# Integer exponentials in groups of four heads from the ninth period on, kept in the space of used-up weights

## The chip, the cores and the metric

One core of a Trainium2 chip runs the whole program. The metric is the device time of one execution in microseconds (us). Engines are named as in the profile: PE (TensorE, with its weight loads as PEld), DVE (VectorE), ACT (ScalarE), POOL (GpSimd), SP (SyncE, which issues DMAs).

## The reference

Two attentions over the same 2048 tokens, mixed by a gate per token (32 heads of 16, bfloat16 inputs):

```python
g = sigmoid((x * gate_w).sum(-1, keepdims=True))      # x: 1 x 2048 x 512
a = A_ref(x, A_wqkv, A_wo)      # full softmax attention
b = B_ref(x, B_wqkv, B_wo)      # 8 keys per query: s, s-2, ..., s-14
return g * a + (1 - g) * b
# A: qkv = x @ wqkv; p = softmax(q k^T * 16**-0.5); o = p v; o @ wo
# B: the same over the 8 gathered keys; keys before token 0 are masked
```

## The kernel before

**Branch A** is the bulk: 32 heads x 2048 x 2048 exponentials. The work goes in periods: a chunk of 512 queries times a group of four heads, 4 x 8 = 32 periods (the last one is split in two halves, so 33 entries). A period has 64 blocks of 128 keys by 512 queries, one head each. PE forms the scores of a block in PSUM (`ring`, two buffers of 3 and 2 blocks), ACT takes the exponential of 3 or 2 blocks at once into `pT`, and PE multiplies `pT` with the values into the period's accumulator (`acc`), where an extra column of ones sums the denominators. The four heads of a period use four 32-wide strips of the PE array, so products for different heads run side by side.

**Blocks on DVE.** In each period `n_dve` of the 64 blocks (3 to 16, 12 in periods 8 to 26) do not go to ACT. PE puts their scores into a shared PSUM bank (`dq`), DVE turns them into 16-bit integers that, read as bfloat16, are a piecewise linear exponential (`p1`, one instruction per block into the tile `dt`), and three more integer instructions per group of blocks add 32, 64 and 96 to those integers (`sh`, from `dt` into `pd_a`). PE multiplies all four versions with differently weighted values (`dpv`: `vp_all` for the first, `vd_all` for the others), which corrects the linear error. The constants: `NV` = 4 versions, `NGR` = 3 blocks in a group, `NGF` = 4 blocks from period `FLAT0` = 27 on, `NPD` = 3 buffers of `pd_a`, `NDL` = 3 buffers of `dt`, `LATE0` = 8 the period from which the late buffers of `dt` are used.

The passes `sh` have two forms. In a group of three the destination rows are padded (`ROW` = 514 columns for 512) and the source is read in half rows: 1536 columns. From period 27 on source and destination are contiguous: 2048 columns in one run (`flat`). The integers lie in `dt_a` in the early periods, in `dt_a` and two parts of `wkv` (A's key and value weights, used up by then) in periods 8 to 26, and in three parts of `bw` (B's weights) from period 27 on, where the first groups wait for the last projections out of `bw` (`bw_users`).

**Branch B** works in 16 tiles of 128 tokens (`b_tile`). PE projects keys, values and queries out of `bw`; SP stores keys and values in DRAM (`kv_scr`) and loads them back shifted (`ksh`, `vsh`); POOL multiplies and sums the logits (`prod`, `lg`); DVE finds the maximum and the sum of the exponentials, ACT the exponentials; POOL scales them, multiplies with the values and adds up (`av`, `obb`), partly by accumulating DMAs from its own queue. PE transposes `obb` (`fin`), DVE stores it in `obt`, and the output projection takes `obt` and A's `oat` together. POOL also divides A's results by their denominators (`rden`, `ott`).

**The order.** Every piece of work is an `Op` with an engine, a planned duration, a due time and its dependences. `list_schedule` plays a timetable with these durations, picks at each step what is due first among what can start, and the instructions of all engines are emitted in that order; each engine then keeps its order on the chip and waits by semaphores. Durations may have parts marked `True`: those occupy a port that the plan shares between DVE and POOL, one at a time. A POOL operation is (0.14 us, then some 0.5 us on the port); a padded pass is entirely off the port; a contiguous pass is given by `PT`. Results of POOL are planned with 4 us of margin before PE uses them and 3 us before DVE or ACT does (`MARGIN`). `BT` are the due times of B's tiles: `b_start`, then a step of `b_space` each. PE's gaps are filled with products of zeros (`zeros`).

Every engine's calls go through one helper, so the profile shows line 370 for nearly all operations and line 379 for the matmuls; the tiles' names tell them apart.

Of the kernel before, what the change touches and what calls it, by code (L numbers as in the profile page):

```python
# [12 lines left out]
BF16 = mybir.dt.bfloat16  # L13
# [6 lines left out]
    n_dve=(3, 3, 6, 6, 9, 9, 12, 12) + (12,) * 19 + (16,) * 4 + (8, 4),  # L20
    dve_tiles=4,
    b_start=36.0,
    b_space=(43.0,) * 16,
    chain=("pe", "dve", "act", "pool", "sp"),
)

# [1 line left out]
DH = 16  # L28
NG = 8
W = 8  # L30
DIL = 2
QW = 512
NEG = -1.0e9
FLAT0 = 27
BITS = 128.0
LN2 = 0.6931471805599453
SHIFT = 175.0
# [1 line left out]
NV = 4  # L39
NGR = 3  # L40
NGF = 4
NK1 = 2
# [7 lines left out]
NDE = 1  # L50
NDL = 3
# [57 lines left out]
PVU, PVN = 100.0, 4  # L109
GP = lambda kind, n: [(False, PRE), (True, NS[kind] * n)]  # L110
SB = lambda n: [(True, 0.065 + n / 3840.0)]
PT = lambda n: [(True, 0.1 + n / 3840.0)]
TT = lambda n: [(True, 0.075 + n / 960.0)]
PASS, SWITCH, KEEP, RIDE, ALONE = 0.22, 0.1, 1.2, 50.0, 3.0
WAIT, FREE, LATE, CLAMP = 0.15, 0.1, 10.0, -1.0
# [192 lines left out]
def kernel(  # L308
# [19 lines left out]
    DC = D // 128  # L328
# [6 lines left out]
    const = ctx.enter_context(tc.tile_pool(name="const", bufs=1))  # L335
# [95 lines left out]
    for pi in range(NP):  # L431
        first_unit.append(nu)
        n = n_dve[pi]
        gr = group_of(pi)
# [16 lines left out]
    for pi, (own, groups) in enumerate(seq):  # L451
        n = sum(len(g) for g in groups)
# [22 lines left out]

    wkv = const.tile([128, DC, 2 * D], BF16, name="wkv")
    wq = const.tile([128, DC, D], BF16, name="wq")
    wq2 = const.tile([128, DC, 8, 2, DH], BF16, name="wq2")
    q_scr = tc.dram_tile([NG * NC // 2 * 16, DH * QW], BF16, name="q_scr")
    wk3 = const.tile([128, DC, NK1, 2, DH], BF16, name="wk3")  # L480
    a_w3 = A_wqkv.rearrange("(c p) n -> p c n", p=128)
    wkp = const.tile([128, DC, (NG - NK1) // 2, 4, 2, DH], BF16, name="wkp")
    gw = const.tile([128, DC], BF16, name="gw")
    bw = const.tile([128, DC, 3 * D], BF16, name="bw")
    bwo = const.tile([128, DC, D], BF16, name="bwo")
# [22 lines left out]
    wkv_l = wkv[:].rearrange("p c n -> p (c n)")  # L508
    dt_bufs = [dt_a[:, k_ * NGR * QW:(k_ + 1) * NGR * QW] for k_ in range(NDE)]
# [319 lines left out]
    for h0, h1, pn in ((4, 8, 1), (8, 16, 2), (16, 24, 4), (24, 32, 6)):  # L829
        TB = 512 // ((h1 - h0) * DH)  # L830
        for tb in range(0, NT, TB):
            late = tb + TB > NT - NTD
# [3 lines left out]
    qt_tiles, o_q, q_tok, last_q = {}, {}, {}, [None]  # L836
# [120 lines left out]
    a = None  # L957
    for sc in range(NC):
        a = op("pe", 0.9, zmm(sc), GT + sc, full=1, deps=[o_bw, a] + o_xt[sc], alloc=[tzp] if sc == 0 else [],
               use=[tzp] if sc else [], rel=20.0)  # L960
    a = op("act", 0.25, zsig, GT + 5, deps=[a], use=[tzp])
    o_g = op("dve", 0.8, zgate, GT + 6, deps=[a])
    a = op("pe", 1.2, zrows, GT + 8, full=1, deps=[o_g, o_init_p], alloc=[tzr])
    o_gr = op("dve", 0.12, zcopy, GT + 9, deps=[a], use=[tzr])


    o_kvd, o_obt, bw_users = [], [], []
    obt_tiles, obt_tok = {}, {}
    WP = WH // 2
    HB = D // 2  # L970
# [1 line left out]
    def b_tile(t):  # L972
# [27 lines left out]
        a = op("pe", WAVE(2), proj("pk", 1, 0), tb - 34 - KB, full=2, deps=[o_bw] + o_xt[cb], alloc=[tk, tkv], rel=rel)  # L1000
        a = op("pe", WAVE(2), proj("pk", 1, 2), tb - 33.5 - KB, full=2, deps=[a], use=[tk])
        ka = op("dve", 0.61, ke, tb - 33 - KB, deps=[a], use=[tk, tkv])
        tk = tok("misc", 2)
        a = op("pe", WAVE(2), proj("pv", 2, 0), tb - 32 - KB, full=2, deps=[o_bw] + o_xt[cb], alloc=[tk], rel=rel, after=[a])
        a = op("pe", WAVE(2), proj("pv", 2, 2), tb - 31.5 - KB, full=2, deps=[a], use=[tk])
# [4 lines left out]

        def qe():
            V.tensor_scalar(out=st["qb"][:], in0=st["pq"][:], scalar1=float(DH) ** -0.5, scalar2=None, op0=ALU.mult)
        bw_users.append(a)
        tk = tok("misc", 2)
        a = op("pe", WAVE(2), proj("pq", 0, 0), tb - 24 - QB, full=2, deps=[o_bw] + o_xt[cb], alloc=[tk, tqb], rel=rel)
        a = op("pe", WAVE(2), proj("pq", 0, 2), tb - 23.5 - QB, full=2, deps=[a], use=[tk])
        bw_users.append(a)
        qa = op("dve", 0.61, qe, tb - 23 - QB, deps=[a], use=[tk, tqb])

        def load(key, off, hf):  # L1020
# [154 lines left out]
        for g_ in range(len(halves)):  # L1175
# [5 lines left out]
        a = op("dve", 0.34, sm_pre, tb + SMD, deps=[l1], use=[tlg])  # L1181
        a = op("dve", 0.0, sm_sub, tb + SMD, deps=[a], use=[tlg], parts=TT(H * W)) if SM_V else op(
            "pool", 0.0, sm_sub, GFIRST, deps=[a], use=[tlg], parts=GP("ff", H * W))
        a.lat += 0.0 if SM_V else 3.0
        l1.lat += SM_LAT[0]
        a = op("act", 0.36, sm_exp, tb + SMD, deps=[a], use=[tlg], lat=0.36 + SM_LAT[2])
        a = op("dve", 0.72, sm_post, tb + SMD, deps=[a], use=[tlg])
# [122 lines left out]
                pv_run(pend[q_:min(n, q_ + 4)], tn)  # L1310
            del pend[:n]

    bw_l = bw[:].rearrange("p c n -> p (c n)")
    wkv_users = [o for o in ops if o.eng == "pe" and o.name.startswith(("kp", "vp"))]
    d_st, d_last, d_sh = {}, [None, None], []
    d_count, d_ends = [0, 0, 0, 0], []
# [1 line left out]
    def d_set(pi, gi, t, j, qk_, tn):  # L1318

        c_, i = periods[pi]  # L1320
        late = pi >= LATE0
        flat, gr = pi >= FLAT0, group_of(pi)
        key = (pi, gi)
        first = key not in d_st
        if first:
            slot = d_count[3] % NDL if flat else d_count[0] % NDL if late else d_count[2] % NDE
            d_count[3] += flat
            d_count[0] += late and not flat
            d_count[2] += not late
            d_st[key] = dict(dt=bw_l[:, slot * gr * QW:(slot + 1) * gr * QW] if flat else dt_bufs[slot],  # L1330
                             td=tok("dtf", NDL) if flat else tok("dtl", NDL) if late else tok("dt", NDE), js=[], ts=[], p1=[])
        g = d_st[key]
        n_ = len(g["js"])
        g["js"].append(j)
        g["ts"].append(t)

        st = {}
        tx = tok("misc", 2)

        def dq():  # L1340
            st["x"] = misc_ps([128, QW])
            for t_, cs in parts_of(pi, t):
                mm(st["x"][:, cs], kt_all[32 * j:32 * j + 32, i, t_ * 128:(t_ + 1) * 128], qt_tiles[pi][32 * j:32 * j + 32, q_cols(pi)],
                   True, True, tile_position=(32 * j, 0))

        def p1():
            V.tensor_scalar(out=g["dt"][:, n_ * QW:(n_ + 1) * QW].bitcast(U16), in0=st["x"][:], scalar1=float(DH) ** -0.5 * BITS / LN2,
                            scalar2=(127.0 + DEXP + SHIFT * float(DH) ** -0.5 / LN2) * BITS, op0=ALU.mult, op1=ALU.add)
        deps = [o_q[pi], o_k[i][tiles_of(pi, t)[0] // TPC]] + [o_vd[(4 * i + j, t_)] for t_ in tiles_of(pi, t)]
        if first and flat and d_count[3] <= NDL:  # L1350
            deps += bw_users
        elif first and late and d_count[0] <= NDL:
            deps += wkv_users + d_ends[-NV * NDE:]
        a = op("pe", 0.0, dq, tn - 3.0, mode="r", js=[j], deps=deps, alloc=[tx] + ([g["td"]] if first else []),
               use=[q_tok[pi]] + ([] if first else [g["td"]]), after=[qk_, d_last[1]], ride=True, name=f"dq{pi}")
        d_last[1] = a
        o = op("dve", 0.61, p1, tn + P1D, deps=[a], use=[tx, g["td"]], after=[d_last[0]], name=f"p1_{pi}")
        d_last[0] = o
        g["p1"].append(o)
        if len(g["js"]) < gr:  # L1360
            return
        vs = [o_vd[(4 * i + j_, t2)] for t_, j_ in zip(g["ts"], g["js"]) for t2 in tiles_of(pi, t_)]

        def sh(m, pb):
            def s():
                o_, i_ = pb.bitcast(U16)[:, :, 0:QW], g["dt"].bitcast(U16)
                if not flat:
                    i_ = _ap(i_, [list(i_.ap[0]), [QW // 2, 2 * NGR], [1, QW // 2]])
                else:
                    o_ = o_.rearrange("p q n -> p (q n)")  # L1370
                V.tensor_scalar(out=o_, in0=i_, scalar1=STEP * m, scalar2=None, op0=ALU.add)
            return s

        def pv(m, pb):
            def s():
                pv_mm(pi, [(t_, j_, pb[:, n1, 0:QW]) for n1, (t_, j_) in enumerate(zip(g["ts"], g["js"]))],
                      lambda t2: vd_all[:, m - 1, t2 - (NT - NTD)] if m else vp_all[:, t2])
            return s

        def dpv(m, pb, deps, use, dl):  # L1380
            b = op("pe", 0.0, pv(m, pb), dl, mode="c", js=g["js"], full=1, deps=deps + [o_t0[pi]] + vs,
                   use=[use, acc_tok[pi]], name=f"dpv{pi}")
            o_pv[pi].append(b)
            d_ends.append(b)
        dpv(0, g["dt"].rearrange("p (q n) -> p q n", q=gr), list(g["p1"]), g["td"], tn + 4.5)
        for m in range(1, NV):
            pb = pd_bufs[d_count[1] % NPD]
            if flat:
                k0 = d_count[1] % NPD * gr * QW
                pb = pd_a[:, k0:k0 + gr * QW].rearrange("p (q n) -> p q n", q=gr)  # L1390
            d_count[1] += 1
            tp = tok("pd", NPD)
            a = op("dve", 0.0, sh(m, pb), tn + 1.5 + SHD * (m - 1), deps=list(g["p1"]), alloc=[tp], use=[g["td"]],
                   lat=(0.065 + NGR * QW / 1920.0 if not flat else 0.1 + gr * QW / 3840.0) + SH_LAT, after=d_sh[-1:],
                   parts=[(False, 0.065 + NGR * QW / 1920.0)] if not flat else PT(gr * QW), name=f"sh{pi}")
            d_sh.append(a)
            dpv(m, pb, [a], tp, tn + 4.5 + SHD * m)

    pend, dwait = [], []
    for k, us in enumerate(sets):  # L1400
        ring = "rA" if k % 2 == 0 else "rB"
        n = len(us)
# [211 lines left out]
```

## Time and profile before

| | |
|---|---|
| median of 3 runs | 800.21 us (799.62 to 801.82) |
| profiled execution: time | 803.18 us |
| profiled execution: span, first to last instruction | 800.3 us |
| busy: PE, DVE, ACT, POOL | 741.5, 692.6, 774.5, 644.3 us |
| mean granted TensorE clock | 0.998 |
| ACT: exponentials of branch A, 128x1536 and 128x1024 | 337 at 1538 ns, 336 at 1117 ns |
| DVE: padded passes of 128x1536 / contiguous of 128x2048 | 288 at 940 ns / 57 at 744 ns |
| POOL: last sum of branch B | starts at 722.2 us |
| ACT: last exponential | ends near 793 us |

Durations of ACT overlap a little, since an instruction starts before the one ahead of it has ended; busy time counts the overlap once. A group's mean can mix shapes, where the profile says so. A wait is put down to the last semaphore that came.

### The profile page before, as it was taken

The numbers are of one execution on the slowest core, as the hardware profiler recorded it, in microseconds if no ns is written. First come the engines' busy times: TensorE is split into PE (matmuls) and PEld (weight loads), VectorE is DVE, ScalarE is ACT, GpSimd is POOL, SyncE is SP. The second block draws the span as 40 slices with busy tenths as digits, with TensorE's granted clock in tenths as the row PEclk, the third lists the DMA queues.
The fourth block names the chain that finished last, engine by engine and source line by source line (L and its number), as shares of the span: only waits on it lengthen the run. The fifth ranks groups of instructions, "written<-read, shape, count | busy, mean of one in ns | idle before, by whom it ended". The sixth has DMA issues, their size and how long they took to land.

```text
span 800.3 us, 17773 instructions
## 1 busy us (share of the span) xinstructions
PE 741.5 (93%) x6817; PEld 241.9 (30%) x6876; DVE 692.6 (87%) x1100; ACT 774.5 (97%) x697; POOL 644.3 (81%) x1067
## 2 busy tenths in 40 slices
PE   8999989999999999999999999998999999999997
PEld 4333333233222222222222232232232232222233
DVE  5638787998887899999998899899898999988986
ACT  3999999999999999999999999999999999999996
POOL 4098989899999997899989899999989999991000
PEclk9999999999999999999999999999999999999999
DMA  8413071625344535336352626253625371100000
GB/s 265 115 46 106 21 177 47 156 64 128 98 113 118 131 83 143 81 97 142 73 146 77 162 74 165 66 117 112 144 65 109 107 169 35 47 8 20 2 2 28
DMA packets 58886, 77.21 MB, mean 96 GB/s; under 512 B 3744, under 2 KB 50848, under 8 KB 58800
## 3 DMA queue, kind: packets, MB, share of 16 engines
q1 hardware_dynamic: 52608, 53.91, 21.6%
q0 software_dynamic: 6048, 22.02, 14.8%
q8 instruction: 53, 0.87, 0.4%
q14 instruction: 33, 0.27, 0.1%
q10 hardware_dynamic: 144, 0.13, 0.0%
HBM read 43.78 MB, written 10.26 MB: 68 GB/s over the span
## 4 chain that ended last, share of the span: by engine, by line
ACT 50%; PE 23%; issue 22%; DVE 4%; DMA 1%; SPq 0%; ACTq 0%; DVEq 0%
ACT pT L370 49%; PE misc_ps L379 15%; PE ring L379 7%; DVE pd_a L370 1%; DMA xld<-in_A_x_dram 1%; DVE dt_a L370 1%; ACT lg L370 1%; DVE vd_all L370 1%; DVE wkv L370 0%; DVE kt_all L370 0%; PE pxt L647 0%; DVE vp_all L370 0%; DVE ssum L370 0%; DVE rr L370 0%; DVE osb L370 0%
## 5 line engine op out<-in xcount | busy, mean ns | idle before, releaser
L370 ACT ACTIVATE pT<-ring 128x1536 bf16<-128x1536 f32 (+1 forms) x674 | 766.5, 1327 | 10.5 <-PE ring L379 7.3
L379 PE MATMUL ring<-qt,kt_all 32*128 32x512 bf16 (+1 forms) x1736 | 265.5, 375 | 41.3 <-ACT pT L370 32.8
L379 PE MATMUL misc_ps<-pT,vp_all 128*17 128x512 bf16 (+3 forms) x1736 | 201.9, 377 | 0.3 <-DVE dt_a L370 0.2
L370 POOL TENSOR_TENSOR prod<-ksh,qb 128x256 f32<-128x256 bf16 x256 | 175.7, 757 | 30.0 <-DMA ksh<-kv_scr 27.2
L379 PEld LDWEIGHTS <-kt_all 32*128 32x128 bf16 x2112 | 92.2, 91 | 291.2 <-issue 281.6
L370 POOL TENSOR_TENSOR prod<-prod 128x256 f32<-128x256 f32 (+1 forms) x256 | 172.8, 690 | 5.9
L370 DVE TENSOR_SCALAR pd_a<-wkv 128x1536 uint16<-128x1536 uint16 x150 | 137.2, 940 | 1.0 <-PE misc_ps L379 0.6
L379 PE MATMUL misc_ps<-qt,kt_all 32*128 32x512 bf16 (+1 forms) x376 | 130.5, 374 | 3.8 <-DVE dt_a L370 2.2
L379 PE MATMUL misc_ps<-pd_a,vd_all 128*17 128x512 bf16 (+1 forms) x1128 | 131.1, 375 | 0.5 <-DVE pd_a L370 0.4
L379 PE MATMUL misc_ps<-z 128*32 128x512 bf16 x382 | 127.9, 388 | 1.6 <-DVE z L370 1.6
L370 DVE TENSOR_SCALAR pd_a<-dt_a 128x1536 uint16<-128x1536 uint16 x138 | 126.5, 939 | 0.6
L370 DVE TENSOR_SCALAR wkv<-misc_ps 128x512 uint16<-128x512 f32 x150 | 100.1, 681 | 18.5 <-PE misc_ps L379 17.6
L370 DVE TENSOR_SCALAR dt_a<-misc_ps 128x512 uint16<-128x512 f32 x138 | 92.1, 682 | 21.0 <-PE misc_ps L379 19.6
L370 POOL TENSOR_TENSOR prod<-vsh,lg 128x256 f32<-128x256 bf16 x128 | 84.1, 772 | 0.0
L379 PEld LDWEIGHTS <-vp_all 128*17 128x17 bf16 (+1 forms) x2112 | 55.9, 88 | 84.8 <-issue 71.9
L370 POOL TENSOR_TENSOR av<-vsh,lg 128x256 f32<-128x256 bf16 x128 | 80.0, 664 | 0.0
L370 DVE TENSOR_SCALAR bw<-misc_ps 128x512 uint16<-128x512 f32 x76 | 50.8, 684 | 10.8 <-PE misc_ps L379 10.2
L379 PE MATMUL misc_ps<-bw,xT 128*128 128x512 bf16 x163 | 50.6, 384 | 1.9 <-issue 1.4
L379 PEld LDWEIGHTS <-vd_all 128*17 128x17 bf16 x1128 | 34.9, 88 | 53.4 <-issue 46.6
L379 PEld LDWEIGHTS <-z 128*32 128x32 bf16 x382 | 32.9, 96 | 45.5 <-issue 26.5
L370 DVE TENSOR_SCALAR pd_a<-bw 128x2048 uint16<-128x2048 uint16 x57 | 41.2, 744 | 0.1
L370 POOL TENSOR_TENSOR rden<-rden,g_rw 128x16 f32<-128x16 f32 x30 | 9.3, 310 | 37.5 <-DVE rden L370 37.4
(100 smaller groups left out, 596.0 us busy)
## 6 DMA issues: line engine op xcount, KB each, us to landing
ksh<-kv_scr SPq DMA_DIRECT2D x32, 512.0 KB
vsh<-kv_scr SPq DMA_DIRECT2D x32, 512.0 KB
av<-prod POOLq DMA_DIRECT2D x28, 512.0 KB, 6.2
av<-av POOLq DMA_DIRECT2D x14, 512.0 KB, 5.0
kv_scr<-kvs SPq DMA_DIRECT2D x16, 256.0 KB
qt<-q_scr SPq DMA_DIRECT2D x30, 128.0 KB
out_dram<-osb SPq DMA_DIRECT2D x15, 128.0 KB
xld<-in_A_x_dram SPq DMA_DIRECT2D x3, 512.0 KB
```

The lines of the kernel that those rows point to most:

```text
L370: return chain_on(key, f(*a, **k))
L379: return chain(nc.tensor.matmul(out, lhsT=lhsT, rhs=rhs, start=start, stop=stop, **kw))
```

## The change

Periods 8 to 26 now work as those from 27 on did: their 12 blocks make three groups of four instead of four groups of three, and their passes are contiguous. `FLAT0` becomes 8. The integers of these and of all later groups lie in three parts of 2048 columns: two in `wkv`, which fill it, and one in a new tile `wx`, which holds what were `wq2` and `wkp` (copies of A's query and key weights) one behind the other. `bw` is no longer used for this, and the wait for its last users goes; the first three groups wait instead for the last projections out of A's weights, for the queries of period 1, and for the last early groups. `n_dve` is unchanged. The plan's cost `PT` of a contiguous pass changes from 0.633 us, all on the shared port, to 0.5 us off it and 0.25 us on it. The steps between B's due times become 45 us instead of 43 after the fourth tile.

```diff
-    b_space=(43.0,) * 16,
+    b_space=(43.0,) * 4 + (45.0,) * 12,
...
-FLAT0 = 27
+FLAT0 = 8
...
-PT = lambda n: [(True, 0.1 + n / 3840.0)]
+PT = lambda n: [(False, 0.5), (True, 0.25)]
...
-    wq2 = const.tile([128, DC, 8, 2, DH], BF16, name="wq2")
+    n_q2, n_kp = DC * 8 * 2 * DH, DC * (NG - NK1) // 2 * 8 * DH
+    wx = const.tile([128, n_q2 + n_kp], BF16, name="wx")
+    wq2 = wx[:, 0:n_q2].rearrange("p (c h e d) -> p c h e d", c=DC, h=8, e=2)
+    wkp = wx[:, n_q2:n_q2 + n_kp].rearrange("p (c i j e d) -> p c i j e d", c=DC, i=(NG - NK1) // 2, j=4, e=2)
...
-    wkp = const.tile([128, DC, (NG - NK1) // 2, 4, 2, DH], BF16, name="wkp")
...
-    bw_l = bw[:].rearrange("p c n -> p (c n)")
+    dt_flat = [wkv_l[:, 0:NGF * QW], wkv_l[:, NGF * QW:2 * NGF * QW], wx[:, 0:NGF * QW]]
...
-            d_st[key] = dict(dt=bw_l[:, slot * gr * QW:(slot + 1) * gr * QW] if flat else dt_bufs[slot],
+            d_st[key] = dict(dt=dt_flat[slot] if flat else dt_bufs[slot],
...
-        if first and flat and d_count[3] <= NDL:
-            deps += bw_users
-        elif first and late and d_count[0] <= NDL:
-            deps += wkv_users + d_ends[-NV * NDE:]
+        if first and late and d_count[3 if flat else 0] <= NDL:
+            deps += wkv_users + [o_q[1]] + d_ends[-NV * NDE:]
```

The lines that collected `bw_users` in `b_tile` go as well.

More of the change, by code (lines that the diff above doesn't have):

```diff
@@ L964 @@
     o_gr = op("dve", 0.12, zcopy, GT + 9, deps=[a], use=[tzr])
-    o_kvd, o_obt, bw_users = [], [], []
+    o_kvd, o_obt = [], []
     obt_tiles, obt_tok = {}, {}
@@ L1012, in qe @@
             V.tensor_scalar(out=st["qb"][:], in0=st["pq"][:], scalar1=float(DH) ** -0.5, scalar2=None, op0=ALU.mult)
-        bw_users.append(a)
         tk = tok("misc", 2)
@@ L1016, in b_tile @@
         a = op("pe", WAVE(2), proj("pq", 0, 2), tb - 23.5 - QB, full=2, deps=[a], use=[tk])
-        bw_users.append(a)
         qa = op("dve", 0.61, qe, tb - 23 - QB, deps=[a], use=[tk, tqb])
```

## The prediction

> **What bounds the kernel now.** I read the busy times first, then the costliest groups, then the busy time by stretch. From the page:
>
> ```profile
> PE 741.5 (93%) x6817; PEld 241.9 (30%) x6876; DVE 692.6 (87%) x1100; ACT 774.5 (97%) x697; POOL 644.3 (81%) x1067
> ...
> L370 ACT ACTIVATE pT<-ring 128x1536 bf16<-128x1536 f32 (+1 forms) x674 | 766.5, 1327 | 10.5 <-PE ring L379 7.3
> ...
> L370 DVE TENSOR_SCALAR pd_a<-wkv 128x1536 uint16<-128x1536 uint16 x150 | 137.2, 940 | 1.0 <-PE misc_ps L379 0.6
> ...
> L370 DVE TENSOR_SCALAR pd_a<-dt_a 128x1536 uint16<-128x1536 uint16 x138 | 126.5, 939 | 0.6
> ...
> L370 DVE TENSOR_SCALAR pd_a<-bw 128x2048 uint16<-128x2048 uint16 x57 | 41.2, 744 | 0.1
> ```
>
> ACT computes the exponentials (674 instructions) and almost never waits. The three pd_a groups are the integer passes on DVE: 288 of 1536 columns at 940 ns, 57 contiguous ones of 2048 at 744 ns. The last kind is what the change spreads. By first starts, the changed stretch (periods 8 to 26) runs from about 228 us to 684.7, where the first contiguous pass stands. Busy time by stretch (PE, PEld, DVE, ACT, POOL, then granted clock):
>
> ```profile
> 228.00:684.00 456.00, 423.94 (x3648) 129.12 (x3683) 420.15 (x621) 454.54 (x411) 421.72 (x708) 1.00 0.44 110
> 684.00:708.00 24.00, 22.09 (x212) 7.03 (x205) 22.18 (x32) 23.95 (x23) 23.01 (x30) 1.00 0.08 27
> 708.00:724.00 16.00, 15.47 (x123) 3.80 (x123) 12.55 (x22) 14.97 (x14) 14.57 (x21) 0.89 0.03 10
> 724.00:793.00 69.00, 64.91 (x776) 23.65 (x779) 61.16 (x106) 69.00 (x62) 2.33 (x4) 1.00 0.03 7
> ```
>
> ACT is busy 454.54 of 456 us where the change acts; from 228 to 793 its idle time sums to 1.46 + 0.05 + 1.03 + 0 = 2.5 us. The number of exponentials stays, so 2.5 us is about all there is to win. POOL (branch B) is the other full engine: 421.72 of 456, until it ends near 723. What is added to POOL moves its end, or stops those who wait for it.
>
> **What a contiguous pass does to POOL.** Only 684 to 724 has both at once. One POOL multiply in 228 to 684.5, and then in 684.5 to 721 (behind the bar: busy us, mean ns):
>
> ```profile
> L370 POOL TENSOR_TENSOR av<-vsh,lg 128x256 f32<-128x256 bf16 x88 | 53.4, 647 | 0.0
> ```
> ```profile
> L370 POOL TENSOR_TENSOR av<-vsh,lg 128x256 f32<-128x256 bf16 x8 | 7.1, 926 | 0.0
> ```
>
> Those eight on the timeline (start, us), and DVE beside them:
>
> ```profile
> 698.04 7.13 POOL L370 TENSOR_TENSOR av<-vsh,lg 128x256 f32<-128x256 bf16 x8
> ```
> ```profile
> 698.60 0.68 DVE L370 TENSOR_SCALAR pd_a<-bw 128x2048 uint16<-128x2048 uint16 x1
> ...
> 699.80 3.23 DVE L370 TENSOR_SCALAR pd_a<-bw 128x2048 uint16<-128x2048 uint16 x3
> ```
>
> A fifth pass starts at 703.54. Eight multiplies take 8 x 647 = 5.18 us undisturbed and 7.13 here: 1.95 over five passes, 0.39 us each; by the means, 8 x (926 - 647) = 2.23, 0.45 each. Over all 16 passes until 721, with every POOL row's mean set against its own of before (12 adds at 799 against 734, and so on), the excess is about 5.3 us, 0.33 each. I take **0.40 us of POOL per pass**, between 0.33 and 0.45, because the changed stretch is as dense in POOL work as this one. The 1536-column passes cost POOL nothing visible: the 647 ns was measured among them.
>
> The same passes from DVE's side, until 721 and after it (minimum/median/maximum ns):
>
> ```profile
> L370 DVE TENSOR_SCALAR pd_a<-bw x16: 629/916/1130, 684.7 to 719.7; 128x2048 uint16<-128x2048 uint16 x16
> ```
> ```profile
> L370 DVE TENSOR_SCALAR pd_a<-bw x41: 629/683/695, 724.0 to 791.0; 128x2048 uint16<-128x2048 uint16 x41
> ```
>
> With POOL at work a pass takes 0.9 us, without it 0.68.
>
> The Trainium skill, SBUF — State Buffer, "Who interferes with whom", says that a VectorE instruction in a two-port mode and a GpSimd instruction lock each other out of a shared port pair, and that the loser is blocked for the whole instruction. The trace agrees on who waits, not on the size: by the page a pass would cost POOL its whole 0.68 us, and the sum below would grow by 171 x 0.28 = 48 us; the rows show 0.33 to 0.45.
>
> **The change part by part.** *Passes on DVE.* Periods 8 to 26 hold 19 x 12 = 228 blocks: 76 groups of three now, 57 groups of four after, three passes each. Out go 228 x 0.940 = 214 us, in come 171 x 0.90 = 154 us: DVE is relieved of 60 us. None of it is on the path, since ACT does not wait there.
>
> *Products on PE.* A group's four products take one turn of the array each, with three or with four heads side by side: 76 x 4 turns become 57 x 4, 76 fewer. On the timeline such turns follow each other by 0.22 us (737.80, 738.02, 738.24), so PE is freed of 17 us in 456. Its reach is the 2.5 us of ACT's idle time, and part of that has other causes; I book 0.
>
> *Bits in wkv and wx instead of dt_a, wkv and bw.* The first groups wait for the last projections out of wkv and wx. Those are done in the first periods, and passes out of wkv already run from 245 us: 0. The group of four gathers one block more before its passes start; its tiles come in threes as before: 0, and if the three buffers were short, some tenths of a us at a wait now 0.6 us in all ("pd_a<-wkv ... 0.6").
>
> *b_space.* The due times of tiles 5 to 15 move later, by 2 us a tile, 22 us for the last. They order the queues (its projections on PE, its DMAs on SP, its chain on POOL) but hold nothing back, as POOL is full anyway. Cost 0 by themselves, since an output of the last quarter has until 793.
>
> *Contention on POOL.* 171 x 0.40 = **68 us** more POOL work (56 to 77), in an engine with 34 us idle in 456. Of that idle time 7.8 us are waits for its own summing DMAs and 5.7 its own chain; waits for DVE (rden 4.6, mx 3.1, qb 2.0, rr 0.9) sum to 10.6, of which DVE's relief may give back some 3.
>
> *What the order foresees.* All queues are written from one plan, and each engine keeps its order. Up to now the plan charged a contiguous pass 0.633 us of the shared port, more than the 0.33 to 0.45 of the trace; the new PT charges 0.25, less. So each pass leaves POOL 0.15 us (0.08 to 0.20) behind the order that PE and DVE follow: 171 x 0.15 = 26 us by the end of period 26 (14 to 34). What the order leaves as room shows in the sums of a tile and the PE transposes that wait for them:
>
> ```profile
> L1219 PE MATMUL misc_ps<-ident,obb x64: 216/219/230, 130.3 to 734.0; 128*128 128x128 bf16 x64
> L370 POOL TENSOR_TENSOR obb<-av x32: 717/727/742, 121.4 to 722.2; 128x256 bf16<-128x256 f32 x32
> ```
>
> Two sums of 0.73 from 121.4 end at 122.8, 7.5 us before the first transpose; for the last tile 722.9 and 734.0, 11 us. So some 8 us are absorbed. After that the transpose stands at the head of PE's queue with the next score matmuls behind it, and ACT behind those; likewise DVE stops at the maximum over the logits, with the evacuations of scores behind it. PE's score buffers are two, so ACT runs dry within about 2 us.
>
> Sum: 26 - 8 - 3 = **+15 us** (14 - 11 - 3 = 0 to 34 - 7.5 = 27). By POOL alone: 723 + 68 - 3 = 788, and the contiguous passes that now fall before its end instead of after it (some 30 of the 41) add 12: 800. After its last sum come transposes, products, eviction and store, the 7 us from the last exponential (793) to the end: 807 at least. The two agree on the sign. The profiled execution took 803.18 us for a span of 800.3, and 800.21 is the median of the runs; +15 on the median gives **815**.
>
> **The rivals.** *Faster: POOL keeps up.* If a pass cost POOL under 0.25 + 8/171 = 0.30 us, the room of 8 us would hold, PE's 17 free us would fill ACT's gaps, and the end would be 800.2 - 2.5 = 797.7. For it: in the middle of the stretch POOL has short instructions and pauses into which a pass may fall. Against it: 0.33 is the lowest reading. 0.12. *No change:* the lag is absorbed and the gaps stay, 800. 0.09. *The passes are not the fast kind* in their new place: 171 x 2048/1536 x 0.940 = 214 us on DVE, as now, and POOL untouched: 800. The form and the contiguous access are those of the 57 existing ones: 0.02. *The clock falls too:* in 708 to 724 the granted clock was 0.89 and ACT lost 1.03 us, with PE 97% busy. Were each of the last eleven tiles' stops to set off one such spell, it would be 815 + 11 = 826. 0.12.
>
> The Trainium skill, TensorE: Matmul & The Clock Gate, "HAM oscillation", ties the half clock to idle gaps of about 3.4 us, which stops of 1 to 3 us would not reach; the row above, with hardly any gap, shows that it can fall without one, which is why that rival keeps a chance.
>
> **How the numbers follow.** Forecast 0.65 at 815, clock 0.12 at 826, faster 0.12 at 797.7, same 0.11 at 800. Measurements of this kernel tell apart 0.3%, 2.4 us. Slower 0.77, same 0.11, faster 0.12. The range leaves out the faster case and the far end: 799 to 832, that is 815 + 15 with 0.45 a pass and a few spells of low clock, and below it the sum with every bound in its favour.
>
> **What would show it.** In the profile after: 171 more passes of 2048 columns (228 in all), those until POOL's end at 0.9 us; 60 of 1536 left; av<-vsh at 0.75 us or more; POOL's last sum at 785 to 805 instead of 722.9; PE or DVE waiting for POOL by name (obb, lg), and ACT idle by 10 us or more between 400 and 790. I am wrong if POOL's multiplies stay near 650 ns, if POOL ends before 770, or if ACT stays above 99% busy to 790.

## The result and the profile after

The changed kernel takes **852.34 us** (median of 4 runs, 847.73 to 854.20); the kernel before took 800.72 beside it. Ratio 1.064, 95% interval 1.059 to 1.068. The forecast had the sign, but 815 us, with 832 as the end of its range. In e10 and e12 below, one execution each at a lower granted clock than its fellows (0.970 and 0.844) is left out of the times.

The profiled execution has a span of 852.4 us, 52.1 more than before. The first lines of the page, and ACT's group:

```profile
PE 761.1 (89%) x6887; PEld 240.5 (28%) x6945; DVE 692.0 (81%) x1043; ACT 780.1 (92%) x697; POOL 719.0 (84%) x1067
...
L370 ACT ACTIVATE pT<-ring 128x1536 bf16<-128x1536 f32 (+1 forms) x674 | 771.5, 1289 | 57.1 <-PE misc_ps L379 34.6
```

ACT's idle time ahead of the exponentials grows from 10.5 to 57.1 us. That is 46.6 of the 52.1. DVE was to lose 60 us of work and shows 692.0, as before (692.6). The busy times by stretch: 228 to 684 as in the kernel before, from there to POOL's end, and from there to the last exponentials. The columns are those of the table of before (PE, PEld, DVE, ACT, POOL, then granted clock):

```profile
228.00:684.00 456.00, 399.02 (x3306) 115.43 (x3337) 370.22 (x497) 412.00 (x368) 401.70 (x584) 0.95 0.37 95
684.00:824.00 140.00, 127.34 (x1175) 37.41 (x1185) 128.12 (x190) 134.34 (x120) 134.13 (x176) 0.98 0.24 62
824.00:846.00 22.00, 20.47 (x354) 9.38 (x346) 18.79 (x36) 21.62 (x20) 0.00 (x0) 1.00 0.05 15
```

Nobody is full any more in the first of them: ACT falls from 454.54 to 412 of 456, DVE from 420 to 370, PE from 424 to 399, and the granted clock from 1.00 to 0.95. The passes on DVE (minimum/median/maximum ns) show something that the forecast did not have:

```profile
L370 DVE TENSOR_SCALAR pd_a<-wkv x153: 629/862/4547, 238.8 to 843.6; 128x2048 uint16<-128x2048 uint16 x153
L370 DVE TENSOR_SCALAR pd_a<-wx x75: 629/1126/5153, 258.6 to 838.3; 128x2048 uint16<-128x2048 uint16 x75
```

The medians are about the 0.9 us of the forecast. The maxima, 4.5 and 5.2 us, are not in it. Counted in the trace, 23 of the 228 passes last over 1.3 us, 61 us together; the other 205 average 0.92 and reach 1.24. One place on the timeline, POOL, DVE, ACT (an x2 or x4 merges neighbours; the second column is their time together):

```profile
379.85 0.87 POOL L370 DMA_DIRECT2D av<-prod  x1 [0.30 <-POOL prod L370]
380.46 2.71 POOL L370 TENSOR_TENSOR prod<-vsh,lg 128x256 f32<-128x256 bf16 x4
383.47 0.87 POOL L370 DMA_DIRECT2D av<-prod  x1 [0.30 <-POOL prod L370]
384.08 2.83 POOL L370 TENSOR_TENSOR prod<-ksh,qb 128x256 f32<-128x256 bf16 x4
386.59 2.79 POOL L370 TENSOR_TENSOR prod<-prod 128x256 f32<-128x256 f32 x3
```
```profile
381.80 7.01 DVE L370 TENSOR_SCALAR pd_a<-wx 128x2048 uint16<-128x2048 uint16 x2
388.73 0.68 DVE L370 TENSOR_SCALAR qb<-misc_ps 128x512 bf16<-128x512 f32 x1
```
```profile
391.31 1.02 ACT L370 ACTIVATE pT<-ring 128x1024 bf16<-128x1024 f32 x1 [4.41 <-PE misc_ps L379]
```

POOL issues a summing DMA at 379.85 and another at 383.47. Two passes, started at 381.80 and 383.65, take 7 us together instead of 1.4 to 1.8. The first ends at 383.73: POOL has paused for 0.30 us ahead of the second DMA, from 383.18 on. The second ends at 388.81, behind four multiplies and two additions that POOL ran without a gap; the third addition starts after a gap of 0.08 us at 388.25. Of the 23 long passes 20 end like this, 0.55 to 0.57 us after a gap in POOL begins; for the other three the trace shows no such gap. PE stands at the products of these passes, and ACT goes dry for 4.41 us. All 23 start 0.2 to 2.7 us behind such a DMA; only 8 other passes start that close, and of the 197 further away none is long. From the waits of the kernel after, and the same line of the kernel before:

```profile
PE misc_ps L379 <- DVE pd_a L370: 32.4, 31, 4.1
```
```profile
PE misc_ps L379 <- DVE pd_a L370: 0.4, 2, 0.2
```

The waits of PE's weight loads for POOL stay small (2.0 us, 1.5 before): the last transposes still come 7 us behind the last sum, which ends at 823.6 us now.

### The profile page after: what moved, and what is told of

Read it like the earlier page. It is cut to its first block, busy times and chain, and to the rows that moved or that the text cites. A ratio compares the mean times of both kernels' runs of the same rounds, so it can differ in the third digit from the quotient of the medians.

```text
span 852.4 us, 17831 instructions
## 1 busy us (share of the span) xinstructions
PE 761.1 (89%) x6887; PEld 240.5 (28%) x6945; DVE 692.0 (81%) x1043; ACT 780.1 (92%) x697; POOL 719.0 (84%) x1067
## 4 chain that ended last, share of the span: by engine, by line
ACT 35%; PE 25%; DVE 20%; issue 18%; DMA 1%; SPq 0%; ACTq 0%; DVEq 0%
ACT pT L370 35%; PE misc_ps L379 17%; DVE pd_a L370 12%; PE ring L379 7%; DVE wkv L370 3%; DVE wx L370 2%; DMA xld<-in_A_x_dram 1%; DVE kvs L370 1%; DVE vd_all L370 1%; DVE kt_all L370 0%; DVE osb L370 0%; PE pxt L649 0%; DVE dt_a L370 0%; DVE qb L370 0%; DVE ssum L370 0%
## 5 line engine op out<-in xcount | busy, mean ns | idle before, releaser
L370 ACT ACTIVATE pT<-ring 128x1536 bf16<-128x1536 f32 (+1 forms) x674 | 771.5, 1289 | 57.1 <-PE misc_ps L379 34.6
L370 POOL TENSOR_TENSOR prod<-ksh,qb 128x256 f32<-128x256 bf16 x256 | 195.5, 834 | 26.9 <-DMA ksh<-kv_scr 26.1
L370 POOL TENSOR_TENSOR prod<-prod 128x256 f32<-128x256 f32 (+1 forms) x256 | 195.3, 775 | 5.3
L370 DVE TENSOR_SCALAR wkv<-misc_ps 128x512 uint16<-128x512 f32 x204 | 136.5, 681 | 49.4 <-PE misc_ps L379 47.7
L370 DVE TENSOR_SCALAR pd_a<-wkv 128x2048 uint16<-128x2048 uint16 x153 | 159.1, 1058 | 0.8
L379 PE MATMUL misc_ps<-z 128*32 128x512 bf16 (+1 forms) x451 | 148.9, 390 | 1.8 <-DVE z L370 1.6
L370 DVE TENSOR_SCALAR pd_a<-wx 128x2048 uint16<-128x2048 uint16 x75 | 84.9, 1166 | 3.8 <-PE misc_ps L379 3.3
L370 DVE TENSOR_SCALAR wx<-misc_ps 128x512 uint16<-128x512 f32 x100 | 67.0, 681 | 18.6 <-PE misc_ps L379 18.2
L370 DVE TENSOR_SCALAR pd_a<-dt_a 128x1536 uint16<-128x1536 uint16 x60 | 54.6, 942 | 0.4
L370 DVE TENSOR_SCALAR dt_a<-misc_ps 128x512 uint16<-128x512 f32 x60 | 39.9, 684 | 14.2 <-PE misc_ps L379 13.4
L379 PEld LDWEIGHTS <-xT 128*128 128x128 bf16 x576 | 29.5, 98 | 37.2 <-issue 34.3
```

Source lines behind the costliest of these rows:

```text
L370: return chain_on(key, f(*a, **k))
L379: return chain(nc.tensor.matmul(out, lhsT=lhsT, rhs=rhs, start=start, stop=stop, **kw))
```

## The experiments

Two theories. **A**, the forecast's: a contiguous pass takes 0.4 us from POOL, the order counts 0.25, and the lag ends as waits for POOL. **B**, from the trace after: behind a DMA that POOL issues, POOL leaves no opening for a while, the pass on DVE waits up to 5 us, and PE and ACT wait behind it. Ratios are against the kernel before, with the 95% interval.

**e1: no DMA from POOL, same order.**

```diff
-  G.dma_start(out=av[:, wp:wp + WP, :], in_=st["av", wp][:], accum_op=ALU.add)
+  G.tensor_tensor(out=av[:, wp, 0:HB], in0=av[:, wp, 0:HB], in1=st["av", wp][:, 0, 0:HB], op=ALU.add)
```

(and likewise for the sum within `av`). An addition covers 256 columns alone, so most of B's sums are left out.

> The changed kernel, same order, with each of POOL's 42 accumulating DMAs replaced by one POOL addition over 256 columns (so only a quarter of one of the sums of branch B is added; the rest is left out). Theory A (the forecast's: POOL is slowed 0.4 us per contiguous pass and the order does not foresee it): the passes still alternate with POOL, nothing changes but some tenths of a us per DMA, 845 to 855 us. Theory B (behind a DMA issued by POOL its next instructions follow one another without an opening, and a contiguous pass on DVE waits up to 5 us): passes over 1.3 us fall from 23 to under 5, ACT's idle time before its exponentials from 57 to under 30 us, the time to 805 to 820 us, the rest over 800 being theory A's share.

Measured 807.23 us, 1.0065 (1.0043 to 1.0086): 45 of the 51 us gone. The longest passes:

```profile
L370 DVE TENSOR_SCALAR pd_a<-wkv x153: 630/966/1267, 238.4 to 797.6; 128x2048 uint16<-128x2048 uint16 x153
L370 DVE TENSOR_SCALAR pd_a<-wx x75: 631/1125/1223, 257.8 to 792.3; 128x2048 uint16<-128x2048 uint16 x75
```

None over 1.27 us; the clock is 0.997 instead of 0.967; PE waits for POOL no longer than in the kernel before. POOL did not get less to do, and DVE is now relieved (first line of the page, beside 719.0 and 692.0 in the kernel after):

```profile
PE 743.8 (92%) x6887; PEld 239.8 (30%) x6945; DVE 661.5 (82%) x1043; ACT 777.3 (96%) x697; POOL 720.3 (89%) x1067
```

Nor had POOL waited long for the DMAs to land (2.9 us in the kernel after). Theory B.

**e2: a wait of POOL for itself behind each DMA, same order.**

```diff
   G.dma_start(...)
+  G.tensor_copy(out=brk[:, 0:1], in_=rowc[:, 0:1])
+  G.tensor_copy(out=brk[:, 1:2], in_=brk[:, 0:1])
```

> The changed kernel, same order, with two one-column copies on POOL behind each of its accumulating DMAs, the second reading what the first wrote, so that POOL waits once for its own result. Theory B in the form that POOL's queue runs ahead behind a DMA: the wait opens a gap, passes over 1.3 us fall from 23 to under 8 and the time to 805 to 825 us, although POOL has some 42 x 0.5 = 21 us more to do. Theory B in the form that writing the descriptors itself holds the shared port for some 4 us: still 20 or more long passes, 845 to 860 us. Theory A: slower than the changed kernel by up to 20 us, since POOL has more work.

833.23 us, 1.039 (1.035 to 1.043). No pass over 1.25 us, with all 42 DMAs in place, so issuing them does not block by itself:

```profile
L370 DVE TENSOR_SCALAR pd_a<-wkv x153: 629/805/1243, 238.3 to 823.2; 128x2048 uint16<-128x2048 uint16 x153
```

But the time fell only by 19, and theory A's waits appeared, POOL having more to do (busy 734.1 us):

```profile
PE misc_ps L1223 <- POOL obb L370: 12.2, 13, 2.8
```

**e10: the same copies without the dependence**, so without the wait (`in_=rowc[:, 1:2]` in the second).

> The kernel with the two one-column copies behind each POOL DMA, but the second copy no longer reads what the first wrote, so POOL has the same number of instructions and no wait for its own result. If the wait is what opens the gap: POOL's instructions go on overlapping behind the DMA (0.95 us each, 0.63 apart), 15 or more passes over 1.3 us, 845 us or more. If any short instruction is enough: no long passes, about 830 us as with the wait.

18 passes over 1.3 us are back, up to 4.3:

```profile
L370 DVE TENSOR_SCALAR pd_a<-wx x75: 632/955/4299, 257.8 to 813.3; 128x2048 uint16<-128x2048 uint16 x75
```

So the wait opens the gap, as expected. The time was a miss: 832.94 us (829.14 to 834.83), not 845. The copies shortened the hold-ups (44 us in long passes, not 61). In the place looked at, POOL's multiplies behind the copies no longer overlap (662 ns each, against 958 in the place shown above), and still a pass took 4.3 us beside them; the overlap is a companion and not the cause.

e2 and e10 take the same time, though e2 has no long pass and e10 has 18. In e2 PE waits 12.2 us for POOL's `obb` and DVE 10.5 for its `lg`; e10 shows neither wait. So with POOL this late, taking the hold-ups away won nothing, and waits for POOL stood in their place. What the hold-ups cost is to be read from e1 above and e9 below, where POOL has no extra work.

**e8: e2 with a plan that knows both costs.**

```diff
-PT = lambda n: [(False, 0.5), (True, 0.25)]
+PT = lambda n: [(False, 0.1), (True, n / 3840.0)]
-DMAQ, DMAL = 1.0, 6.0
+DMAQ, DMAL = 1.6, 5.4
```

> The kernel with the two dependent copies behind each POOL DMA, and a plan that knows both costs: a contiguous pass at 0.1 us and 0.533 us on the shared port, and a POOL DMA at 1.6 us instead of 1.0. The copies alone gave 833 us, with PE waiting 12.2 us for POOL's obb. Theory A for that rest: these waits go, and POOL's own length sets the end, 812 to 824 us. If the rest came from elsewhere (the clock, DVE): still 828 us or more.

821.25 us, 1.025 (1.022 to 1.028). ACT runs through, and the end is POOL's:

```profile
L370 ACT ACTIVATE pT<-ring 128x1536 bf16<-128x1536 f32 x337 | 520.7, 1545 | 8.4 <-PE ring L379 6.0 <-PE misc_ps L379 1.7
```
```profile
L370 POOL TENSOR_TENSOR obb<-av x32: 717/729/1245, 121.8 to 808.1; 128x256 bf16<-128x256 f32 x32
```

The last sum begins at 808.1, the last exponential has ended at 791.8, and the span is 818.7. POOL's length sets the end, as in the forecast's lower bound ("807 at least"), here with 84 copies more.

**e4: the plan's cost alone**, `PT` as in e8, no copies.

> The changed kernel with the plan's cost of a contiguous pass raised to 0.1 us and 0.533 us on the shared port (0.4 us for POOL, as measured), so the order foresees the slower POOL. Theory A: the wait for POOL goes, 852 - 25 = 827 us or less, bounded below by POOL's end, about 810. Theory B: the plan still does not know of the waits behind a DMA, 20 or so passes over 1.3 us stay, 840 to 858 us.

842.51 us, 1.051 (1.047 to 1.054), 14 long passes left; ACT idles 37 us ahead of the exponentials instead of 57, and 14 at the end, where the last output waits. A better count of theory A's cost is worth 10 us here.

**e9: the plan keeps contiguous passes away from the DMAs.**

```diff
+HOLD = 3.6
...
+        if e == "dve" and o.name.startswith("sh") and any(sh_ for sh_, _ in o.parts):
+            t = max(t, hold[0])
...
+            if o.far:
+                hold[0] = t + HOLD
```

> The changed kernel with one rule more in the plan: no contiguous pass is planned to start within 3.6 us of a DMA issued by POOL; DVE does other work there. POOL gets nothing more to do. Theory B (a pass that starts behind such a DMA is held up, and PE and ACT behind it): long passes fall from 23 to 8 or fewer, 808 to 825 us. Theory A: 845 to 855 us, as the POOL time per pass stays.

832.14 us, 1.038 (1.035 to 1.041); 12 long passes, 30 us together. Half as many, and 20 us back, less than expected. The 12 start 0.4 to 3.3 us behind a DMA, inside the window of 3.6 that the plan kept free: the real order of the two engines drifts from the planned one.

**e3: padded rows with groups of four.**

> The changed kernel with groups of four and all else, but in periods 8 to 26 the passes go to padded rows of 514 columns with the source in half rows (the form of the kernel before), and the plan has their cost of 1.13 us. Both theories put the loss on the contiguous access: 797 to 806 us, passes at about 1.25 us each, none over 1.5, POOL's multiplies at 650 ns. If groups of four, the place of the bits or the later due times were to blame: 830 us or more.

851.02 us, 1.062 (1.058 to 1.067). A miss, and my design's: the padding does not make the slow kind.

```profile
L370 DVE TENSOR_SCALAR pd_a<-wkv x153: 624/808/4550, 238.5 to 836.3; 128x2048 uint16<-128x2048 uint16 x153
```

Four rows of 512 from eight half rows run as fast as one run of 2048 (0.68 us undisturbed) and are held up alike; three rows from six half rows take 0.94 and are not. The Trainium skill, VectorE: DVE Perf Modes, "What auto-detection actually checks", asks for outermost counts that are both even or equal for a two-port mode: 4 and 8 are, 3 and 6 are not. The rows agree, with these two pairs alone. So the padding was not what made the form before the slow kind; by the page it was the three rows against six.

**e5: groups of three in the new places.** Everything changed but the groups: `FLAT0` = 27, with periods from 8 on taking their slots in `wkv` and `wx`.

> The changed kernel (bits in the key, value and query weights, new due times, new plan cost), but periods 8 to 26 with groups of three and padded passes of 1536 columns as before. All theories that blame the contiguous kind of pass: 797 to 805 us, passes at 0.94 us, none over 1.3 before period 27. If the place of the bits, the waits or the due times carried a part of the 51 us: 810 us or more.

807.88 us (804.95 to 813.10), 1.0095 (1.006 to 1.013), no pass over 1.22 us:

```profile
L370 DVE TENSOR_SCALAR pd_a<-wkv x192: 628/943/1217, 236.9 to 795.7; 128x1536 uint16<-128x1536 uint16 x153, 128x2048 uint16<-128x2048 uint16 x39
```

Nearly all of the loss is gone; 5 to 10 us stay with the new due times, places and plan cost, more than expected. What of these three they come from was not tried.

**e11, e12, e13: contiguity alone, in the order of before.** The kernel before, groups of three, every engine's order unchanged; in e11 and e12 only the access becomes one run of 1536 columns from period 8 on, in e12 and e13 the DMAs are replaced as in e1.

```diff
-                if not flat:
+                if not late:
                     i_ = _ap(i_, [list(i_.ap[0]), [QW // 2, 2 * NGR], [1, QW // 2]])
...
-            if flat:
+            if late:
                 k0 = d_count[1] % NPD * gr * QW
```

> The kernel before, with its own order on every engine, groups of three, due times and places of the bits; only the access of the 228 passes of periods 8 to 26 becomes contiguous (1536 columns in one run). Theory B: the quiet pass falls from 0.94 to about 0.55 us, DVE is relieved of some 60 us, and yet 20 or more passes last over 1.2 us behind POOL's DMAs, PE waits for pd_a, and the time rises to 825 to 860 us. Theory A, POOL's extra 0.3 us per pass alone: POOL ends at about 785 instead of 723, 803 to 820 us. If the order, the groups of four or the new places made the loss: 800 us or less.

> The kernel before with contiguous passes of three as above, and each POOL DMA replaced by one POOL addition over 256 columns (most of branch B's sums are left out). Theory B: no pass over 1.2 us, 798 to 806 us. Theory A: as with the DMAs, less a few us.

> The kernel before with only the POOL DMAs replaced in that way: the control for what their absence is worth where the passes do not contend. ACT sets the time, so 798 to 802 us by all theories; if the DMAs themselves cost the order something, down to 795.

e11: 845.50 us, 1.058 (1.051 to 1.065), with 15 passes over 1.3 us, up to 4.5, 39 us together:

```profile
L370 DVE TENSOR_SCALAR pd_a<-wkv x150: 511/750/4548, 246.4 to 716.8; 128x1536 uint16<-128x1536 uint16 x150
```

A different access pattern in 228 instructions, and nothing else, costs 45 us. e13: 799.63, 0.999 (0.998 to 1.000), so the DMAs are harmless where the passes are of the slow kind. e12 is a miss: 832.28 us (832.25 to 833.37) instead of 806, with no pass over 1.22 us. It differs from e13 by the access alone, so 32 us of loss come without any DMA, and theory A is a real cost: in this order it is the larger part of e11's 45. In e1, where the order counts 0.25 us a pass, 6 us were left. In e11's profile it shows as a wait of DVE for POOL's logits, which e1 and e13 do not have:

```profile
DVE mx L370 <- POOL lg L370: 15.1, 8, 3.7
```

That its price depends on how much of it the order has foreseen is argued from e12 and e1 and not shown: e12 also has 228 changed passes where e1 has 171 more, other groups and other due times.

## Why the prediction was right and wrong

- *ACT has 2.5 us to win, the change cannot be faster.* Right: no version with contiguous passes got below 806 us.
- *0.40 us of POOL per pass.* Right in size. e1 and e13 differ in POOL's busy time by 720.3 - 634.4 = 85.9 us; 216 contiguous passes lie before the last sum of e1 and 16 before that of e13: 85.9 / 200 = 0.43 us. POOL's last sum moves by less, from 720.8 to 776.8, 0.28 a pass, since POOL's idle time ahead of it falls from 89 to 57 us. The lower reading, 0.33, stood on less than the forecast says: the rows that run in both stretches give 3.4 us of the 5.3, 0.21 a pass. The rest can only be the eight additions `av<-av` (961 ns), which run only behind 684 and have no mean of before.
- *The whole 0.68 us per pass*, as the forecast reads the Trainium skill, SBUF — State Buffer, "Who interferes with whom", is too much here too: the difference would be 136 us and was 85.9.
- *Passes on DVE: 171 x 0.90 us, none of it on the path.* **This step failed.** The term was mis-sized: 23 passes took 61 us where 0.92 each makes 21. And its cover, "ACT does not wait there", was gone in the same stroke, since PE keeps its order and stands at the products: 32.4 us where it was 0.4, with ACT's idle time up by 46.6. The price of 0.9 us was read between 684 and 721, where B's last two tiles sum on POOL itself (`t < NT - 2` in `sums_of`). All 42 DMAs of the page lie ahead of that stretch; it had POOL work of the same density and none of the kind that mattered. The trace of before had one sign. DVE's `qa` step, a short instruction over 256 columns, takes 0.28 us where POOL is idle and up to 0.83 beside POOL away from its DMAs. Here it starts 1.1 us behind a DMA and takes 1.40:

```profile
569.54 0.89 POOL L370 DMA_DIRECT2D av<-av  x1
```
```profile
570.60 1.40 DVE L370 TENSOR_SCALAR qa<-qs 128x256 uint32<-128x256 uint32 x1
```

- *The lag ends as waits of PE for POOL.* Not in the kernel after: the hold-ups slowed PE, ACT and DVE until POOL was no longer late, and POOL waited for DVE (25.0 us for `rr`, 3.3 before). The lag came out where the hold-ups were taken away and POOL had yet more to do (e2: 12.2 us), and fell to 5.1 us, 4.8 of them in one wait, when the plan knew of it (e8).
- *POOL alone: 807 at least.* Too high by the 0.40 it took per pass, where POOL's end moves by 0.28: e1's POOL ends at 777.6, not 800. e1's 807.23 agrees with the bound by luck, as its last exponential, at 799.6, sets its end. In e8, with its copies, POOL does set the end, at 821.
- *The clock falls too* (a rival at 0.12, one spell per tile): it did, as a companion. The trace after has 11 spells of half clock between 228 and 824, 55 us in all. Ten of them follow a gap of 1.5 to 4.1 us between PE's matmuls, eight of these gaps under the 3.4 us that the forecast set against this rival; with the stops gone (e1) the clock is back at 0.997. How the 51 us divide between stops and spells was not separated.
- *Bits in other places, due times: 0.* Some 5 to 10 us by e5.

The 51 us, then, in the order of the kernel after: 45 hang on the DMAs of POOL together with contiguous passes (e1). The other 6 are no more than e5 shows for the new order by itself, so no run shows a share of its own for POOL's slower pace there. The sign of the forecast came out right by another path than the one it gave. Of what it named to look for, the passes and ACT's idle time came; the waits for POOL by name did not, and POOL's last sum stands at 822.9, behind its 785 to 805.

## What to carry to other kernels

Before a cost is taken from the one stretch that shows two engines together, list which kinds of instruction each engine runs there and which it runs where the change will act; a kind that is missing has no price yet. An instruction that can be held up by another engine has a longest case as well as a mean, and in queues that keep their order the longest case sets what waits behind it. A fast form that takes a resource from a fuller engine buys nothing: here it was to relieve DVE, which nobody waited for, at the cost of POOL.

## What the runs showed of the hardware that was not expected

A contiguous 16-bit pass on DVE, which beside POOL otherwise lasts 1.27 us at most, can last up to 5.15 us when it starts behind a POOL-issued DMA; in the kernel after, 20 of 23 such passes end 0.55 to 0.57 us after a gap in POOL begins, even one of 0.08 us. Two dependent one-column copies behind the DMA remove all such cases (0 of 228 over 1.25 us), two independent ones do not (18 over 1.3). What inside the engines holds the pass up is not shown. Among passes of 16-bit integers, four rows from eight half rows take 0.68 us for 2048 columns and are held up (e3: up to 5.15 us); three rows from six take 0.94 for 1536 and are not (0.89 to 0.96 for all 288 of the kernel before).
